# Spectral mixing and SwiGLU on one core: the first batch's first Fourier step kept in SBUF, re/im interleaved in the intermediates, last sums on VectorE

## The chip, the cores and the metric

The kernel runs on one NeuronCore of a Trainium2 chip. The metric is the device time of one execution in microseconds, as a median over runs. Before the change it is 3045.3 us (3043.2 to 3047.6, 3 runs).

## The reference, cut to what matters

```python
def _attn_ref(x, filt_r, filt_i):            # x: 8 x 3008 x 256
    X = np.fft.rfft(x, axis=1)
    Y = X * (filt_r + 1j * filt_i)[None]
    return np.fft.irfft(Y, n=x.shape[1], axis=1).astype(np.float32)

def _moe_ref(x, w_gate, w_val, w_out):       # 24064 tokens, 256 -> 1536 -> 256
    g = x @ w_gate
    return ((g / (1.0 + np.exp(-g))) * (x @ w_val) @ w_out).astype(np.float32)
```

The weights come in as float64. The kernel rounds them to float32 itself, in 36 "halves" of 128 x 256 numbers.

## The kernel before: the parts concerned

The transform of a batch runs in steps of matmuls: step one over 47 points, middle steps (a, product with the filter, b) over 64 points for 24 frequencies in 12 units of two, and the last step, which yields `y`. Between them stand two intermediates in DRAM, `d1` and `d2`. Batch one does all this before the main part can start; for batches two to eight the same steps are woven into the products of the batch before, each in the schedule of a group (one round of gate, value and output products).

```python
        def stage1(self, u):                      # step one, 16 of them
            ...
            pin(nc.tensor.matmul(out=ps[0:NK], lhsT=wf_t, rhs=self.x.pop(u), ...))
            yield
            pin(nc.scalar.copy(out=t1, in_=ps[0:NK]))
            queue = nc.scalar if self.b else nc.gpsimd
            pin(queue.dma_start(out=self.d1_rows[:, ts(u, NV), :], in_=t1))

        def load_two(self, u):                    # input of the middle steps
            ...
            for p in range(2):                    # real part, imaginary part
                a0 = p * NS + NV * u
                self.load(out=self.t2[u][64 * p:64 * p + 64],
                          in_=self.d1[a0:a0 + NV].rearrange("s n c -> n s c"))

        def stage2b(self, u):                     # end of the middle steps
            ...
            pin(nc.scalar.copy(out=g, in_=ps))
            for p in range(2):
                a0 = p * NS + NV * u
                queue = nc.scalar if self.b else (nc.sync, nc.gpsimd)[p]
                pin(queue.dma_start(out=self.d2[a0:a0 + NV].rearrange("s n c -> n s c"),
                                    in_=g[64 * p:64 * p + 64]))
```

For the later batches the two stores of `stage2b` stand in ScalarE's own order.

A rounding takes VectorE (two bit operations), ScalarE (two activations), VectorE again (three operations) and GpSimd (two to four), with its two intermediates `pw` and `w`.

In the lines of the profile PE is TensorE, PEld its weight loads, DVE VectorE, ACT ScalarE, POOL GpSimd and SP SyncE; a q behind the name means the engine's sequencer. `out<-in` names the tiles. `wpa` to `wpd` (`pa` to `pd` for later batches) are results of the Fourier steps, `wk`, `wa` and `we` those of the gate and value products, `wA`, `wF` and `wG` those of the output products; `f`, `c`, `m` and `o` are copies of such results (`f` with its sign changed) that ScalarE makes; `room`, `t` and `lent` are buffers in SBUF, `d` the intermediates in DRAM.

Of the kernel before, what the change touches and what calls it, by code (L numbers as in the profile page):

```python
# [93 lines left out]

LAST = "W1 o1 W2 o2 W6 o6 W5 o5 W3 o3 x0.o x1.o x2.o W7 o7 W4 o4 x3.o x4.o x5.o".split()
BLOCKS = (0, 1, 3, 2)
# [11 lines left out]
def dft_tables():  # L108
# [3 lines left out]
    w = np.stack([np.cos(ph), -np.sin(ph)], 1)  # L112
    wf = np.zeros((N1, 2, 2, NS, 2))
    wi = np.zeros((2, NS, 2, N1, 2))

    v = np.stack([2 * np.cos(ph), -2 * np.sin(ph)], 0)
    v[0, :, 0], v[1, :, 0] = 1.0, 0.0
    for h in range(2):
        wf[:, h, :, :, h] = w
        wi[:, :, h, :, h] = v.transpose(0, 2, 1) / S  # L120

# [18 lines left out]
def kernel(  # L140
# [13 lines left out]
    wi_dram = nc.inline_tensor(wi_host, name="wi_tbl")  # L154
    de_dram = nc.inline_tensor(de_host, name="de_tbl").ap()

    def pool(name, bufs, space=None):
# [36 lines left out]

    off_t = cpool.tile([128, 1], FP32)
    nc.vector.memset(off_t, -896.0)

    def filter_parts():
# [53 lines left out]
    NRAW = 3  # L252
    N_EARLY = 8

    def load_weights(i):
        if i in raws or i >= len(weights):
            return
        if i < N_EARLY:
            raws[i] = early_raw(i)
        else:  # L260
            raws[i] = rpool.tile([128, 2, 128, 2], U32, name=f"raw_{i}", tag="raw", bufs=NRAW)
        queue = nc.sync if i < N_EARLY else nc.scalar
        pin(queue.dma_start(out=raws[i], in_=weights[i][0]))

    def round_half(i):
# [14 lines left out]
        pin(nc.scalar.activation(out=w, in_=man, func=AF.Copy, scale=2.0 ** -20, bias=1.0))  # L280
        pin(nc.scalar.activation(out=pw, in_=pw, func=AF.Relu, bias=off_t))

        load_weights(i + NRAW - 1)
        yield
        pin(v.tensor_scalar(out=pw, in0=pw, scalar1=255.0, scalar2=2.0 ** 23,
                            op0=ALU.min, op1=ALU.mult))
        pin(v.scalar_tensor_tensor(out=pw.rearrange(flat), in0=raw.rearrange(flat2)[:, :, 1],
# [5 lines left out]
        e = nc.gpsimd  # L293
        pf = pw.bitcast(FP32)
        if use == "proj":
# [73 lines left out]
    def fbank(name):  # L369
        return fps.tile([128, NV, C], FP32, name=name, tag="f")  # L370

    def warm():


        banks = [bank("idle") for _ in range(NB)]
        for n in (512, 512, TQ, 2 * TQ):
            for ps in banks:
                pin(nc.tensor.matmul(
                    out=ps[:, 0:n], lhsT=wt_t[:, 0, 0, :],
                    rhs=wt_t[:, 0:2].rearrange("p s z f -> p (s z f)")[:, 0:n],  # L380
                    start=True, stop=True))

    class Spectral:
# [10 lines left out]
        def load(self, **kw):  # L394
            pin(nc.sync.dma_start(**kw))

        def place(self, tag, u):
            return lend(tag, u) if self.b else early(tag, u)

        def load_x(self, u):  # L400
            if self.b == 0:
                rows = x[0].rearrange("(r n) c -> r n c", n=32)
                for a, n in ((0, NV), (NV, 8 - NV)) if u == 0 else ((0, 8),):
                    for r in (slice(0, 80), slice(80, NR)):
                        self.load(out=x0[u][r, a:a + n, :],
                                  in_=rows[r, 8 * u + a:8 * u + a + n, :])
                for j in range(8 // NV):
                    self.x[8 // NV * u + j] = x0[u][:, ts(j, NV), :]
            elif u < N_ONE:
                self.x[u] = xpool.tile([NR, NV, C], FP32, name=f"x_{self.b}_{u}", tag="x")  # L410
                rows = x[self.b].rearrange("(r n) c -> r n c", n=32)

                for r in (slice(0, 80), slice(80, NR)):
                    self.load(out=self.x[u][r], in_=rows[r, ts(u, NV), :])

        def load_two(self, u):
            if u < N_TWO:
                b = self.b
                if b:
                    self.tb[u] = lend("tb", u).rearrange("p i (k c) -> p i k c", k=2)  # L420
                    self.load(out=self.tb[u], in_=de_dram[:, ts(u, NV)])

                    f = lend("f", u).rearrange("p (k i) c -> p k i c", k=2)
                    self.f[u] = f
                    for rows, view in filter_parts():
                        r, part = rows.start, rows.start // 64
                        for at in (r, r + 64) if part == 0 else (r,):
                            self.load(out=f[at:at + 32, part], in_=view(NV * u, NV))
                self.t2[u] = self.place("t2", u)
                for p in range(2):  # L430
                    a0 = p * NS + NV * u
                    self.load(out=self.t2[u][64 * p:64 * p + 64],
                              in_=self.d1[a0:a0 + NV].rearrange("s n c -> n s c"))

# [19 lines left out]
        def stage1(self, u):  # L454

            p1 = spool0 if self.b == 0 and u % 2 else t1pool
            t1 = p1.tile([NK, NV, C], FP32, name=f"t1_{self.b}_{u}", tag="t1", bufs=2)
            ps = self.bank(f"pa_{self.b}_{u}")
            pin(nc.tensor.matmul(out=ps[0:NK], lhsT=wf_t, rhs=self.x.pop(u),  # L459
                                         start=True, stop=True))  # L460
            if self.b:
                self.load_x(u + 3)
            yield
            pin(nc.scalar.copy(out=t1, in_=ps[0:NK]))
            queue = nc.scalar if self.b else nc.gpsimd
            pin(queue.dma_start(out=self.d1_rows[:, ts(u, NV), :], in_=t1))

        def stage2a(self, u):

            ahead = 1 if self.b else 3  # L470
            self.load_two(u + ahead)
            t2, f = self.t2.pop(u), self.f.pop(u)
# [25 lines left out]
        def stage2b(self, u):  # L498
# [8 lines left out]
            pin(nc.scalar.copy(out=g, in_=ps))  # L507
            for p in range(2):
                a0 = p * NS + NV * u
                queue = nc.scalar if self.b else (nc.sync, nc.gpsimd)[p]  # L510
                pin(queue.dma_start(out=self.d2[a0:a0 + NV].rearrange("s n c -> n s c"),  # L511
                                    in_=g[64 * p:64 * p + 64]))

# [52 lines left out]
    class Group:  # L566
# [89 lines left out]
        def project(self, op, last=False):  # L656
# [3 lines left out]
            if kind == "x":  # L660
                if q == NG - 1:
                    i, t = divmod(p, len(TOK))
                    skip = TOK[1] + 128 - TOK[2] if t == 2 else 0
                    rows = out[b * S:(b + 1) * S].rearrange("(r n) c -> r n c", n=32)
                    queue = (nc.sync, nc.scalar, nc.gpsimd)[t] if last else nc.gpsimd
                    pin(queue.dma_start(
# [40 lines left out]
    with tc.tile_pool(name="start", bufs=1) as spool0:  # L707
# [6 lines left out]
        units += [y_f[:, ts(i, NV * C)].rearrange("p (i c) -> p i c", c=C) for i in range(6)]  # L714
        early_places = {"p": (0, 5), "t2": (5, 4), "g": (9, 4), "q": (13, 3), "fr": (16, 3)}

# [4 lines left out]
        def early_raw(i):  # L721

            t, a = (tb0, i) if i < 4 else (f0, i - 4)
            t = t[:, 16 + 2 * a:18 + 2 * a]
            t = t.rearrange("p s k f -> p (s k f)" if i < 4 else "p s c -> p (s c)")
            return t.bitcast(U32).rearrange("p (b f two) -> p b f two", b=2, two=2)

        pin(nc.sync.dma_start(out=wf_t, in_=wf_dram.ap()))
        for i, n in enumerate((0, 2, 2, 4)):
            spec.load_x(i)  # L730
            for _ in range(n):
                load_weights(len(raws))
        for i in range(2):
            spec.load_tables(i)
        pin(nc.sync.dma_start(out=wi_t, in_=wi_dram.ap()))
        for u in range(N_ONE):
            run(spec.stage1(u))
            if u in (7, 8, 10, 11, 13, 14, 15):
                round_next()
        for _ in range(2):  # L740
            round_next()
        for u in range(3):
            spec.load_two(u)
        spec.load_tables(2)
        for i, j in PAIRS:
            combine_weights(0, i, j)
        for u in range(3):
            spec.real_part(u)
        lag = 3
        for u in range(N_TWO + lag):  # L750
            if u < N_TWO:
                run(spec.stage2a(u))
                spec.real_part(u + 3)
            if u >= lag:
                run(spec.stage2b(u - lag))
    for i in range(2):
        spec.load_t4(0, i)
    following = Spectral(1)
    for u in range(3):
        following.load_x(u)  # L760
    warm()
    for _ in range(8):
        round_next()
    for step in range(4):
# [3 lines left out]
    for piece in range(len(PIECES)):  # L768
        keep_weights(0, piece)

    hpool = pool("hp", 4)
# [7 lines left out]
    for b in range(B):  # L779
# [26 lines left out]
        for step in range(NCHUNK * NG + (b == B - 1)):  # L806
# [19 lines left out]
            for token in SCHEDULE:  # L826
# [12 lines left out]
                else:  # L839
                    g0 = before if old else this  # L840
                    if g0 is not None:
                        g0.step(op, nc.vector if ghost and op[0] == "S" and op[2] == "1" else None)
                if old or this is None:
# [19 lines left out]
    for op in LAST:  # L863
        older.project(op, True)
# [28 lines left out]
```

## Time and profile before

| part of the span | from, to (us) | length |
|---|---|---|
| start, up to the first product of the third group | 0 to 212.5 | 212.5 |
| steady stretch, up to the first of the last output products | 212.5 to 3017.9 | 2805.3 |
| last output products and sums | 3017.9 to 3032.9 | 15.0 |
| from the last sum to the end of the span | 3032.9 to 3043.3 | 10.4 |

Two lines of TensorE in order of time (start, duration, engine, line, operation, tiles, shapes, count) give the two cuts of the steady stretch before:

```profile
212.54 0.80 PE L600 MATMUL wk<-y,wt_t 128*128 128x188 f32 x4
...
3017.85 1.50 PE L677 MATMUL wA<-wo_t,h 128*128 128x128 f32 x12
```

### The profile page before, as it was taken

How to read it: one execution, taken by the hardware profiler on the slowest of the kernel's cores; microseconds unless marked ns; L12 is line 12 of the kernel's file. 1: busy time of each engine (PE TensorE's matmuls, PEld its weight loads, DVE VectorE, ACT ScalarE, POOL GpSimd, SP SyncE). 2: the span in 40 equal slices, each digit the busy share in tenths (PEclk: the TensorE clock that was granted, in tenths of full speed). 3: DMA queues.
4: the chain of work that ended last, by engine and by line, in shares of the span. 5: the costliest groups of instructions: out<-in, count | busy, mean ns of one | idle time of the engine just before them, and what ended most of it. 6: DMA issues, size and time to landing. Idle time of an engine off the chain costs nothing.

```text
span 3043.3 us, 57524 instructions
## 1 busy us (share of the span) xinstructions
PE 2948.7 (97%) x20152; PEld 2827.3 (93%) x20152; DVE 1923.5 (63%) x4407; ACT 1581.1 (52%) x4130; POOL 1599.7 (53%) x1797
## 2 busy tenths in 40 slices
PE   5779999999999999999999999999999999999998
PEld 2579999999999999999999999999999999999997
DVE  4686766566665666557665576655666566666665
ACT  3455455555455555555555545555545555555553
POOL 4665655454645455545554555545554545555553
PEclk9889999999999999999999999999999999999999
DMA  8645755556645656456655575555665566644442
GB/s 235 184 143 198 225 185 180 177 189 192 210 154 185 200 191 209 152 185 205 195 173 186 172 227 175 181 182 181 204 203 160 178 199 192 196 147 154 144 131 72
DMA packets 209739, 551.76 MB, mean 181 GB/s; under 512 B 32502, under 2 KB 104438, under 8 KB 208594
## 3 DMA queue, kind: packets, MB, share of 16 engines
q1 hardware_dynamic: 155724, 467.57, 48.5%
q10 hardware_dynamic: 43104, 51.66, 5.9%
q0 software_dynamic: 10624, 28.85, 3.0%
q8 instruction: 162, 2.65, 0.4%
q14 instruction: 125, 1.02, 0.1%
HBM read 462.76 MB, written 85.20 MB: 180 GB/s over the span
## 4 chain that ended last, share of the span: by engine, by line
PE 89%; ACT 1%; issue 1%; DMA 1%; DVE 1%; POOL 1%; ACTq 0%; POOLq 0%; DVEq 0%
PE wa L600 23%; PE wA L677 16%; PE wk L600 15%; PE we L600 12%; PE wG L677 8%; PE wF L677 4%; PE pd L522 3%; PE pa L459 3%; PE pb L476 2%; PE pc L503 2%; DMA out_dram<-o 1%; ACTq L511 0%; ACT lent L507 0%; POOL h L213 0%; ACT y_t L561 0%
## 5 line engine op out<-in xcount | busy, mean ns | idle before, releaser
L600 PE MATMUL wa<-y_t,wt_t 128*128 128x188 f32 x4560 | 902.5, 324 | 7.4 <-ACT wa L626 4.7
L600 PEld LDWEIGHTS wa<-y_t,wt_t 128*128 128x128 f32 x4560 | 749.0, 191 | 34.1 <-issue 15.8
L213 POOL TENSOR_TENSOR h<-h 128x376 f32<-128x376 f32 x191 | 183.4, 981 | 834.9 <-DVE h L647 834.9
L600 PE MATMUL wk<-y,wt_t 128*128 128x188 f32 x3040 | 586.2, 326 | 17.4 <-ACT f L615 11.4
L677 PE MATMUL wA<-wo_t,h 128*128 128x128 f32 x4608 | 580.0, 276 | 9.5 <-DVE o L213 6.1
L677 PEld LDWEIGHTS wA<-wo_t,h 128*128 128x128 f32 x4608 | 564.2, 192 | 24.3 <-issue 14.4
L216 POOL TENSOR_TENSOR h<-h 128x376 f32<-128x376 f32 x573 | 556.9, 993 | 0.6
L600 PEld LDWEIGHTS wk<-y,wt_t 128*128 128x128 f32 x3040 | 493.2, 192 | 49.9 <-issue 22.6
L600 PE MATMUL we<-y_t,wt_t 128*128 128x188 f32 x2280 | 441.4, 323 | 0.0
L216 DVE TENSOR_TENSOR we<-we,m 128x376 f32<-128x376 f32 x576 | 318.2, 555 | 186.9 <-PE we L600 128.4
L600 PEld LDWEIGHTS we<-y_t,wt_t 128*128 128x128 f32 x2280 | 377.1, 190 | 1.3 <-DVE we L220 0.7
L220 DVE SCALAR_TENSOR_TENSOR y<-wk,c 128x376 f32<-128x376 f32 x480 | 244.5, 542 | 153.6 <-ACT we L631 104.3
L216 POOL TENSOR_TENSOR D<-f,f 128x376 f32<-128x376 f32 x288 | 279.8, 985 | 113.7 <-ACT f L615 113.0
L635 ACT COPY m<-wa 128x376 f32<-128x376 f32 x576 | 272.7, 473 | 77.9 <-PE wa L600 76.8
L642 ACT ACTIVATE g<-wa 128x188 f32<-128x188 f32 x576 | 187.1, 327 | 200.4 <-PE wa L600 199.6
L677 PE MATMUL wG<-wo_t,h 128*128 128x128 f32 x2304 | 288.8, 275 | 0.7 <-DVE o L213 0.7
L677 PEld LDWEIGHTS wG<-wo_t,h 128*128 128x128 f32 x2304 | 282.1, 192 | 0.9 <-issue 0.9
L642 ACT ACTIVATE u<-we 128x188 f32<-128x188 f32 x576 | 189.4, 329 | 177.7 <-DVE we L216 157.2
L615 ACT ACTIVATE f<-wk 128x376 f32<-128x376 f32 x288 | 139.9, 486 | 253.9 <-PE wk L600 214.3
L622 DVE SCALAR_TENSOR_TENSOR x<-wk,f 128x376 f32<-128x376 f32 x192 | 104.5, 544 | 237.4 <-PE wk L600 236.5
L619 ACT COPY c<-wk 128x376 f32<-128x376 f32 x288 | 136.3, 473 | 223.7 <-PE wk L600 222.1
L631 ACT COPY we<-y 128x376 f32<-128x376 f32 x480 | 223.5, 487 | 50.6 <-issue 28.2
(119 smaller groups left out, 3833.6 us busy)
## 6 DMA issues: line engine op xcount, KB each, us to landing
wt_t<-w_all SPq DMA_DIRECT2D x186, 896.0 KB
wt_t<-w_all SPq DMA_DIRECT2D x186, 768.0 KB
t<-d SPq DMA_DIRECT2D x64, 384.0 KB
d<-t ACTq DMA_DIRECT2D x112, 192.0 KB
lent<-de_tbl SPq DMA_DIRECT2D x84, 256.0 KB
lent<-in_filt_r_dram SPq DMA_DIRECT2D x336, 64.0 KB
lent<-d SPq DMA_DIRECT2D x168, 128.0 KB
d<-lent ACTq DMA_DIRECT2D x168, 128.0 KB
```

Of the source, the lines that this page charges most:

```text
L213: return eng.tensor_tensor(out=dst, in0=a, in1=b, op=ALU.add)
L216: return eng.tensor_tensor(out=dst, in0=a, in1=b, op=ALU.subtract)
L220: return nc.vector.scalar_tensor_tensor(out=dst, in0=a, scalar=-1.0, in1=b, op0=ALU.mult, op1=ALU.subtract)
L459: pin(nc.tensor.matmul(out=ps[0:NK], lhsT=wf_t, rhs=self.x.pop(u), start=True, stop=True))
L600: pin(nc.tensor.matmul(out=ps[:, z], lhsT=self.wt[:, SLOT[p], z], rhs=rhs, start=start and z == 0, stop=True, skip_group_check=True))
L615: pin(act.mul(self.small(f"f{i}", f"f{i}", 1), t[f"k{i}"], -1.0))
L619: pin(act.copy(out=self.small(f"c{i}", f"c{i}", 1), in_=t[f"k{i}"]))
L622: pin(v.scalar_tensor_tensor(out=dst, in0=t[f"k{j}"], scalar=-1.0, in1=t[f"f{i}" if j == 3 else f"D{at}"], op0=ALU.mult, op1=ALU.add))
L631: pin(act.copy(out=self.bank(f"e{at}"), in_=t[f"y{at}"]))
L635: pin(act.copy(out=self.small(f"m{at}", "m", 4), in_=t[f"a{at}"]))
L642: pin(act.activation(out=self.small(op, "g", 3, 1)[:, 0], in_=ps[:, 1], func=AF.Silu))
L677: pin(nc.tensor.matmul(out=self.tiles[at][:, t, :], lhsT=self.hs[i][:, HID[p], t0:t0 + 128], rhs=wo_t[:, JB * q + i, WO[p], :], start=star ...
```

## The change

Its aim is the start: the first batch's intermediate `d1` no longer goes to DRAM and back. Step one is done with operands swapped, so that channels lie on partitions; the result stays in SBUF, and TensorE transposes it for the middle steps. SBUF so freed and DMA so spared let raw weights be loaded further ahead; roundings and weight combinations are reordered, and one rounding operation moves from VectorE to ScalarE. Since the transposes want real and imaginary part of one frequency side by side, both intermediates are laid out that way for all batches, and a unit's two transfers of 64 partitions become one of 128. At the end the eight last sums go to VectorE and the last stores to the two hardware queues.

```diff
+        def twos(self, d, u):
+            a = 2 * NV * u
+            return d[a:a + 2 * NV].rearrange("(s p) n c -> s (p n) c", p=2).rearrange(
+                "s q c -> q s c")
 ... load_two (batches two to eight)
-                for p in range(2):
-                    a0 = p * NS + NV * u
-                    self.load(out=self.t2[u][64 * p:64 * p + 64],
-                              in_=self.d1[a0:a0 + NV].rearrange("s n c -> n s c"))
+                self.load(out=self.t2[u], in_=self.twos(self.d1, u))
 ... stage2b
-            for p in range(2):
-                a0 = p * NS + NV * u
-                queue = nc.scalar if self.b else (nc.sync, nc.gpsimd)[p]
-                pin(queue.dma_start(out=self.d2[a0:a0 + NV].rearrange("s n c -> n s c"),
-                                    in_=g[64 * p:64 * p + 64]))
+            queue = nc.scalar if self.b else nc.sync
+            pin(queue.dma_start(out=self.twos(self.d2, u), in_=g))
 ... first batch
+                    pin(nc.tensor.matmul(out=ps[:, i], lhsT=x0[u // 2][:, u % 2 * 4 + i, ts(cb, 128)],
+                                         rhs=wf_t, start=True, stop=True))
 ...
+                    pin(nc.tensor.transpose(out=ps[:, i, ts(cb, 128)],
+                                            in_=one_t[:, cb, ts(NV * u + i, 128)], identity=unit_t))
 ... rounding
-        pin(nc.scalar.activation(out=pw, in_=pw, func=AF.Relu, bias=off_t))
+        pin(nc.scalar.activation(out=pf, in_=pw, func=AF.Relu, bias=off_t))
+        pin(nc.scalar.activation(out=pf, in_=pf, func=AF.Relu, bias=top_t, scale=-1.0))
+        pin(nc.scalar.activation(out=pw, in_=pf, func=AF.Copy, scale=-(2.0 ** 23), ...))
-        pin(v.tensor_scalar(out=pw, in0=pw, scalar1=255.0, scalar2=2.0 ** 23, ...))
 ... last stores
-                    queue = (nc.sync, nc.scalar, nc.gpsimd)[t] if last else nc.gpsimd
+                    queue = (nc.sync, nc.scalar)[(p + i) % 2] if last else nc.gpsimd
 ... (order of the start, early loads of raw weights, idle matmuls, last sums: cut)
```

More of the change, by code (lines that the diff above doesn't have):

```diff
@@ L93 @@
 KS = (-1, 0, 1, 2)
-LAST = "W1 o1 W2 o2 W6 o6 W5 o5 W3 o3 x0.o x1.o x2.o W7 o7 W4 o4 x3.o x4.o x5.o".split()
+LAST = """
+S00 S01 S10 S11 W1 o1 W2 o2 S20 S21 S30 S31 W6 o6 W5 o5 W3 o3 x0.o x1.o x2.o W7 o7 W4 o4 x3.o x4.o
+x5.o
+""".split()
 BLOCKS = (0, 1, 3, 2)
@@ L112, in dft_tables @@
     w = np.stack([np.cos(ph), -np.sin(ph)], 1)
-    wf = np.zeros((N1, 2, 2, NS, 2))
-    wi = np.zeros((2, NS, 2, N1, 2))
+    wf = np.zeros((N1, 2, NS, 2, 2))
+    wi = np.zeros((NS, 2, 2, N1, 2))
     v = np.stack([2 * np.cos(ph), -2 * np.sin(ph)], 0)
@@ L118, in dft_tables @@
     for h in range(2):
-        wf[:, h, :, :, h] = w
-        wi[:, :, h, :, h] = v.transpose(0, 2, 1) / S
+        wf[:, h, :, :, h] = w.transpose(0, 2, 1)
+        wi[:, :, h, :, h] = v.transpose(2, 0, 1) / S
     kap = np.where(q[:, None] < 32, s + N1 * q[:, None], s + N1 * (95 - q[:, None]))
@@ L155 @@
     de_dram = nc.inline_tensor(de_host, name="de_tbl").ap()
+    unit_dram = nc.inline_tensor(np.eye(128, dtype=np.float32), name="unit_tbl")
     def pool(name, bufs, space=None):
@@ L195 @@
     off_t = cpool.tile([128, 1], FP32)
+    top_t = cpool.tile([128, 1], FP32)
     nc.vector.memset(off_t, -896.0)
+    nc.vector.memset(top_t, 255.0)
     def filter_parts():
@@ L252 @@
     NRAW = 3
-    N_EARLY = 8
+    N_EARLY = 16
     def load_weights(i):
@@ L261, in load_weights @@
             raws[i] = rpool.tile([128, 2, 128, 2], U32, name=f"raw_{i}", tag="raw", bufs=NRAW)
-        queue = nc.sync if i < N_EARLY else nc.scalar
+        queue = nc.sync if i < 9 else nc.scalar
         pin(queue.dma_start(out=raws[i], in_=weights[i][0]))
@@ L280, in round_half @@
         pin(nc.scalar.activation(out=w, in_=man, func=AF.Copy, scale=2.0 ** -20, bias=1.0))
-        pin(nc.scalar.activation(out=pw, in_=pw, func=AF.Relu, bias=off_t))
+        pf = pw.bitcast(FP32)
+        pin(nc.scalar.activation(out=pf, in_=pw, func=AF.Relu, bias=off_t))
+        pin(nc.scalar.activation(out=pf, in_=pf, func=AF.Relu, bias=top_t, scale=-1.0))
+        pin(nc.scalar.activation(out=pw, in_=pf, func=AF.Copy, scale=-(2.0 ** 23),
+                                 bias=255 * 2.0 ** 23))
         load_weights(i + NRAW - 1)
         yield
-        pin(v.tensor_scalar(out=pw, in0=pw, scalar1=255.0, scalar2=2.0 ** 23,
-                            op0=ALU.min, op1=ALU.mult))
         pin(v.scalar_tensor_tensor(out=pw.rearrange(flat), in0=raw.rearrange(flat2)[:, :, 1],
@@ L293, in round_half @@
         e = nc.gpsimd
-        pf = pw.bitcast(FP32)
         if use == "proj":
@@ L370, in fbank, with idle @@
         return fps.tile([128, NV, C], FP32, name=name, tag="f")
+    def idle(t, banks, n):
+        for ps in banks:
+            pin(nc.tensor.matmul(out=ps[:, 0:n], lhsT=t[:, 0:128], rhs=t[:, 0:n],
+                                 start=True, stop=True))
     def warm():
         banks = [bank("idle") for _ in range(NB)]
-        for n in (512, 512, TQ, 2 * TQ):
-            for ps in banks:
-                pin(nc.tensor.matmul(
-                    out=ps[:, 0:n], lhsT=wt_t[:, 0, 0, :],
-                    rhs=wt_t[:, 0:2].rearrange("p s z f -> p (s z f)")[:, 0:n],
-                    start=True, stop=True))
+        for n in (TQ, 2 * TQ):
+            idle(wt_t[:, 0:2].rearrange("p s z f -> p (s z f)"), banks, n)
     class Spectral:
@@ L406, in load_x @@
                                   in_=rows[r, 8 * u + a:8 * u + a + n, :])
-                for j in range(8 // NV):
-                    self.x[8 // NV * u + j] = x0[u][:, ts(j, NV), :]
             elif u < N_ONE:
@@ L417, in load_two @@
             if u < N_TWO:
-                b = self.b
-                if b:
-                    self.tb[u] = lend("tb", u).rearrange("p i (k c) -> p i k c", k=2)
-                    self.load(out=self.tb[u], in_=de_dram[:, ts(u, NV)])
-                    f = lend("f", u).rearrange("p (k i) c -> p k i c", k=2)
-                    self.f[u] = f
-                    for rows, view in filter_parts():
-                        r, part = rows.start, rows.start // 64
-                        for at in (r, r + 64) if part == 0 else (r,):
-                            self.load(out=f[at:at + 32, part], in_=view(NV * u, NV))
-                self.t2[u] = self.place("t2", u)
-                for p in range(2):
-                    a0 = p * NS + NV * u
-                    self.load(out=self.t2[u][64 * p:64 * p + 64],
-                              in_=self.d1[a0:a0 + NV].rearrange("s n c -> n s c"))
+                self.tb[u] = lend("tb", u).rearrange("p i (k c) -> p i k c", k=2)
+                self.load(out=self.tb[u], in_=de_dram[:, ts(u, NV)])
+                f = lend("f", u).rearrange("p (k i) c -> p k i c", k=2)
+                self.f[u] = f
+                for rows, view in filter_parts():
+                    r, part = rows.start, rows.start // 64
+                    for at in (r, r + 64) if part == 0 else (r,):
+                        self.load(out=f[at:at + 32, part], in_=view(NV * u, NV))
+                self.t2[u] = lend("t2", u)
+                self.load(out=self.t2[u], in_=self.twos(self.d1, u))
         def load_tables(self, i):
@@ L454, in stage1 @@
         def stage1(self, u):
-            p1 = spool0 if self.b == 0 and u % 2 else t1pool
-            t1 = p1.tile([NK, NV, C], FP32, name=f"t1_{self.b}_{u}", tag="t1", bufs=2)
+            t1 = t1pool.tile([NK, NV, C], FP32, name=f"t1_{self.b}_{u}", tag="t1", bufs=2)
             ps = self.bank(f"pa_{self.b}_{u}")
@@ L460, in stage1, with stage1_first, turn @@
                                          start=True, stop=True))
-            if self.b:
-                self.load_x(u + 3)
+            self.load_x(u + 3)
             yield
             pin(nc.scalar.copy(out=t1, in_=ps[0:NK]))
-            queue = nc.scalar if self.b else nc.gpsimd
-            pin(queue.dma_start(out=self.d1_rows[:, ts(u, NV), :], in_=t1))
+            pin(nc.scalar.dma_start(out=self.d1_rows[:, ts(u, NV), :], in_=t1))
+        def stage1_first(self, u):
+            for cb in range(2):
+                ps = bank(f"pa_{u}_{cb}")[:, 0:4 * NK].rearrange("p (n k) -> p n k", k=NK)
+                for i in range(4):
+                    pin(nc.tensor.matmul(out=ps[:, i], lhsT=x0[u // 2][:, u % 2 * 4 + i, ts(cb, 128)],
+                                         rhs=wf_t, start=True, stop=True))
+                copy = (nc.scalar.copy, nc.vector.tensor_copy)[cb]
+                dst = one_t[:, cb].rearrange("p (k n) -> p n k", n=32)
+                pin(copy(out=dst[:, ts(u, 4)], in_=ps))
+        def turn(self, u):
+            if u >= N_TWO:
+                return
+            ps = self.bank(f"pt_{u}")
+            for i in range(NV):
+                for cb in range(2):
+                    pin(nc.tensor.transpose(out=ps[:, i, ts(cb, 128)],
+                                            in_=one_t[:, cb, ts(NV * u + i, 128)],
+                                            identity=unit_t))
+            self.t2[u] = early("t2", u)
+            pin(nc.scalar.copy(out=self.t2[u], in_=ps))
         def stage2a(self, u):
-            ahead = 1 if self.b else 3
-            self.load_two(u + ahead)
+            if self.b:
+                self.load_two(u + 1)
             t2, f = self.t2.pop(u), self.f.pop(u)
@@ L714 @@
         units += [y_f[:, ts(i, NV * C)].rearrange("p (i c) -> p i c", c=C) for i in range(6)]
-        early_places = {"p": (0, 5), "t2": (5, 4), "g": (9, 4), "q": (13, 3), "fr": (16, 3)}
+        early_places = {"p": (0, 5), "t2": (5, 3), "g": (9, 4), "q": (13, 3), "fr": (16, 3)}
+        zero = units[8].rearrange("p i c -> p (i c)")
+        one_t = lent[:, 0:2 * NK * 32].rearrange("p (b k) -> p b k", b=2)
+        spare = []
+        n = 0
+        while n < NPR - 1:
+            pair = ORDER[n][0] in "ABE" and ORDER[n + 1][0] in "ABE"
+            spare += [n] if pair else []
+            n += 2 if pair else 1
         def early(tag, u):
@@ L721, in early_raw @@
         def early_raw(i):
-            t, a = (tb0, i) if i < 4 else (f0, i - 4)
-            t = t[:, 16 + 2 * a:18 + 2 * a]
-            t = t.rearrange("p s k f -> p (s k f)" if i < 4 else "p s c -> p (s c)")
+            t = wt_t[:, spare[i]:spare[i] + 2].rearrange("p s z f -> p (s z f)") if i < 8 else \
+                wo_f[:, ts(i - 8, 512)]
             return t.bitcast(U32).rearrange("p (b f two) -> p b f two", b=2, two=2)
+        unit_t = spool0.tile([128, 128], FP32, name="unit")
+        pin(nc.scalar.dma_start(out=unit_t, in_=unit_dram.ap()))
+        pin(nc.vector.memset(zero, 0.0))
+        idle(zero, [bank("idle") for _ in range(5)], 512)
         pin(nc.sync.dma_start(out=wf_t, in_=wf_dram.ap()))
@@ L732 @@
                 load_weights(len(raws))
-        for i in range(2):
+        for i in range(3):
             spec.load_tables(i)
         pin(nc.sync.dma_start(out=wi_t, in_=wi_dram.ap()))
-        for u in range(N_ONE):
-            run(spec.stage1(u))
-            if u in (7, 8, 10, 11, 13, 14, 15):
+        for u in range(8):
+            spec.stage1_first(u)
+            if u in (4, 5, 6, 7):
                 round_next()
-        for _ in range(2):
-            round_next()
-        for u in range(3):
-            spec.load_two(u)
-        spec.load_tables(2)
-        for i, j in PAIRS:
-            combine_weights(0, i, j)
+        idle(tb0.rearrange("p s k c -> p (s k c)"), [bank("idle") for _ in range(4)], 512)
+        for u in range(2):
+            spec.turn(u)
         for u in range(3):
             spec.real_part(u)
+        for _ in range(4):
+            round_next()
         lag = 3
@@ L751 @@
             if u < N_TWO:
+                spec.turn(u + 2)
                 run(spec.stage2a(u))
@@ L755 @@
                 run(spec.stage2b(u - lag))
+            if 2 < u < 11:
+                load_weights(len(raws))
     for i in range(2):
@@ L760 @@
         following.load_x(u)
+    for _ in range(3):
+        round_next()
+    for i, j in PAIRS:
+        combine_weights(0, i, j)
+    for _ in range(2):
+        round_next()
     warm()
-    for _ in range(8):
-        round_next()
     for step in range(4):
@@ L769 @@
         keep_weights(0, piece)
+    for _ in range(4):
+        round_next()
     hpool = pool("hp", 4)
@@ L840 @@
                     g0 = before if old else this
-                    if g0 is not None:
-                        g0.step(op, nc.vector if ghost and op[0] == "S" and op[2] == "1" else None)
+                    if g0 is not None and not (ghost and op[0] == "S"):
+                        g0.step(op)
                 if old or this is None:
@@ L863 @@
     for op in LAST:
-        older.project(op, True)
+        if op[0] == "S":
+            older.step(op, nc.vector)
+        else:
+            older.project(op, True)
 _INS = ['x', 'filt_r', 'filt_i', 'moe_w_gate', 'moe_w_val', 'moe_w_out']
```

## The prediction

> **What bounds the kernel now.** I read the page first (busy shares, then the 40 slices), then the stretches of the first 100 us, then each engine in order of time around the places where TensorE stands still, and last the final 30 us.
>
> ```profile
> PE 2948.7 (97%) x20152; PEld 2827.3 (93%) x20152; DVE 1923.5 (63%) x4407; ACT 1581.1 (52%) x4130; POOL 1599.7 (53%) x1797
> PE   5779999999999999999999999999999999999998
> ```
>
> From the fourth slice on (228 us) TensorE is full: that is the steady part, some 2,800 us, whose matmuls the change leaves alone. Only the first three slices and the last can give anything. A complete wait list of TensorE over the first 240 us:
>
> ```profile
> PE wpb L476 <- DMA room<-d: 29.7, 5, 20.3
> PE wk L600 <- ACT f L615: 14.7, 5, 6.5
> PE wpa L459 <- DMA wo_t<-in_x_dram: 7.3, 2, 6.4
> PE wk L600 <- DVE y L213: 6.0, 1, 6.0
> ```
>
> The largest wait, 29.7 us, is what the change is aimed at: the first batch's step one is written to DRAM (d<-t) and read back (room<-d) before the middle steps. In order of time:
>
> ```profile
> 28.12 7.03 PE L459 MATMUL wpa<-x,wf_t 94*96 94x512 f32 x8
> 55.49 4.57 PE L476 MATMUL wpb<-room,tb 128*128 128x256 f32 x12 [20.33 <-DMA room<-d]
> 67.39 2.04 PE L476 MATMUL wpb<-room,tb 128*128 128x256 f32 x4 [7.33 <-DMA room<-d]
> 92.76 18.83 PE L378 MATMUL widle<-wt_t 128*128 128x512 f32 x56
> 121.13 1.62 PE L600 MATMUL wk<-y,wt_t 128*128 128x188 f32 x4 [5.99 <-DVE y L213]
> ```
>
> Step one ends at 35.2, the middle steps start at 55.5, and the first product of the main part at 121.1. But between 92.8 and 121 TensorE does idle work and one short step: somebody else sets the pace. VectorE shows who:
>
> ```profile
> 89.61 0.69 DVE L487 TENSOR_TENSOR y_t<-wpb,f 64x512 f32<-64x512 f32 x1
> 90.33 0.29 DVE L276 TENSOR_SCALAR w<-raw 128x256 uint32<-128x256 uint32 x1
> 106.81 0.29 DVE L276 TENSOR_SCALAR w<-raw 128x256 uint32<-128x256 uint32 x1 [3.04 <-DMA raw<-in_moe_w_gate_dram]
> 114.77 0.29 DVE L276 TENSOR_SCALAR w<-raw 128x256 uint32<-128x256 uint32 x1 [3.14 <-DMA raw<-in_moe_w_gate_dram]
> 120.58 0.49 DVE L213 TENSOR_TENSOR y<-wpd,y 128x188 f32<-128x188 f32 x1 [1.26 <-ACT y L534]
> ```
>
> The middle steps leave VectorE at 90.3; then eight roundings of float64 weight halves go through a VectorE-ScalarE-GpSimd loop until 119.2, and only behind them, in program order, the step that yields y. So the start is bound by a chain: loads, step one, DRAM round trip, middle steps, eight roundings, y, first group. What counts is how far the whole chain moves, not the 20 us gap alone.
>
> **What the Trainium skill says.**
> - "TensorE: Matmul & The Clock Gate", Part 1: after an idle window of about 3.4 us the array runs at half clock until about 3.4 us of activity. The trace agrees: the two passes of a 94x512 matmul start 0.86 us apart in step one, and take 0.86 us together once warm (208.60, the chain of waits). The column of granted clock says 1.00 in step one all the same, so it does not show this state.
> - "DMA: Bandwidth & Descriptors", Specifications: the HBM limit per core is about 358 GB/s. The trace reaches 354 in its best 10 us (20 to 30), with the DMA engines' share at 1.05: the loads of the start run near a limit.
> - "ScalarE: Activation LUTs", What ACT_TABLE_LOAD costs: an ACTIVATE is 186 ns + 0.833 ns per element, and about 93 ns more with a bias from a tile. For 256 elements 399 and 492 ns; the trace has 0.42 and 0.50 us for the two activations of a rounding.
> - "TensorE: Matmul & The Clock Gate", Part 4: a 128x128 transpose in bf16 takes 275 to 390 ns, and transposes do not count as activity for the clock. No run here has one yet, and none of float32.
>
> **The change, part by part.**
>
> *Loads.* The DRAM write (16 x 192 KB = 3.1 MB) and the read back (another 3.1 MB) go. Before the middle steps there remain x 3.1 MB, eight weight halves 2.1 MB and three tables of 2.1 MB, 11.5 MB. The windows give 1.66 MB in the first 10 us and 277 to 354 GB/s after; at an estimated 300, x is in at 1.66 + 0.3(t - 10) = 4.15 (x with four halves), t = 18 us; the first table (7.3 MB) at 29; the last at 43.
>
> *Step one.* 64 matmuls of 96 moving columns with 128 stationary ones, in place of 16 of 512. The nearest row is the last Fourier step, 32 records of 96*128 96x94 in 3.71 us, two for a matmul: 0.23 us each warm. 64 x 0.23 = 15 us, against 27.4 us (32 x 0.857, cold) now. Five idle matmuls at the start hold it warm, but it waits for x: I expect its end at about 22 us instead of 35. That is 13 us, which I do not count, since the next thing waits for the table.
>
> *Start of the middle steps.* Four idle matmuls need the first table (29), then the turns of units 0 and 1 (two copies of 0.58), six copies of the filter's real part (6 x 0.63), which wait for the same table, and then, behind them on ScalarE, four roundings. Those go at the pace of the loop: now 3.07 us each where nothing else waits (95.93 to 99.00). So 29 + 4.5 (idle, half cold) + 1.2 + 3.8 + some 9.5 for the roundings = 48 us for the first VectorE product, which is at 57.9 now.
>
> *Middle steps.* VectorE needs 2.16 us a unit (three products of 0.7). ScalarE now needs per unit 1.26 + 0.59; the change adds the copy of a turn, 0.58, and from unit 3 to 10 a DMA issue of 0.37: 2.8 us, so it becomes the bound in about six units. 3 x 2.16 + 6 x 2.8 + 3 x 2.16 = 30 us. They end at 78 on VectorE instead of 90.3: 12 us gained. The stall of 5 us that the trace has at 64 to 69 (room<-d) is in this.
>
> *Behind them.* Now: eight roundings in 28.9 us, of which 8.0 us are waits for raw weights. After: three roundings, the six weight combinations (on VectorE some 8 us now, at 49.7 to 58, hidden in the DRAM wait; on GpSimd 12 operations of 0.8, so about 9 to 10 us for the pair), then two roundings. With raw weights loaded ahead: 5 x 2.9 + 9 = 23 us. y starts 6 to 7 us sooner relative to the middle steps. But four roundings now come after y, ahead of the first group's VectorE work: 4 x 2.9 = 11.6 us given back. Net -5.
>
> *The rounding itself.* One VectorE operation (0.2 us from start to start) becomes two activations (0.50 + 0.41 us) on ScalarE. The loop VectorE, GpSimd, VectorE gets 0.2 us shorter; ScalarE's extra 0.9 us fits into a round. Over the 19 roundings that fall into the crowded stretch after 126 us, where VectorE is 80% busy, I allow 3 us, with the head start TensorE gets on products that wait for nothing.
>
> *Warming.* 14 idle matmuls of 512 columns go (14 x 0.86 = 12 us of TensorE). TensorE waits for VectorE there, so nothing.
>
> *The end.* Now:
>
> ```profile
> 3023.45 1.58 PE L677 MATMUL wA<-wo_t,h 128*128 128x128 f32 x12 [2.75 <-DVE o L213]
> 3019.10 3.74 DVE L216 TENSOR_TENSOR h<-h 128x376 f32<-128x376 f32 x3
> 3032.31 0.56 DVE L213 TENSOR_TENSOR o<-o,wA 128x384 f32<-128x384 f32 x1 [1.70 <-PE wA L677]
> ```
>
> Four sums on GpSimd (0.98 each) and four on VectorE hold up the output sums and so the third product until 3023.45. All eight on VectorE at 0.47 us from start to start, with the output sums between them: first four done at 3020.4, o1 at 3020.9, W6 at 3020.9 instead of 3023.45. Through o5 (3024.4), W3 (3025.8), o3, W7 (3027.1), o7, W4 (3029.3) the last output sum ends at 3030.1 instead of 3032.9: 2.8 us. The last stores leave GpSimd's queue for the two hardware queues: two issues of 0.6 us on one of them, about even.
>
> *Sum.* -12 (middle steps) + 5 (behind them) - 3 (rounding, head start) - 3 (end) = -13 us. My table landing at 29 us is on the careful side, so I put -15: 3030 us.
>
> **The rivals.**
> 1. *The DRAM trip's gain comes through whole.* If the four early roundings do not sit behind the table and the combinations hide behind GpSimd and ScalarE, the first group starts about 25 us sooner: 3018. For it: 20.3 us of pure wait go. Against: program order on ScalarE, and the combinations lose the wait they were hidden in.
> 2. *Another wait takes its place entirely.* The tables pace the middle steps, or TensorE falls cold between the idle matmuls and the loop, so that eight passes and four transposes take over 4 us a unit for the first few. The middle steps then end near 86, and with +5 behind them only the end is gained: 3040. For it: 11.5 MB at 300 GB/s is 43 us whatever TensorE does; transposes may not keep the clock.
> 3. *ScalarE becomes the bound in the crowded stretch* through its 0.9 us a rounding, delaying f, m and g that TensorE waits for (14.7 us on f now). This would cost up to 19 x 0.9 = 17 us: 3045. Against it: ScalarE's 52% share and its idle times there.
>
> **Range and chances.** The sum's uncertain terms are the start of the middle steps (5 us either way), their pace (4) and the given-back roundings (5); the steady part repeats within 0.2%. 3015 to 3041 us should hold it 8 in 10. A gain of 2% is 61 us, over four times the sum and more than the DRAM waits, y wait and end together, so hardly possible; a loss of 2% would need the steady part to suffer. Faster 0.02, within 2% 0.97, slower 0.01.
>
> **What would show it.** Step one's last matmul near 22 us; no room<-d at all; the first product of the middle steps on VectorE near 48 and its last near 78, with ScalarE full between; combinations between the third and fourth rounding behind them; y near 101; four roundings between y and the first group; third product of the end 2.5 us sooner. Wrong would be: a first middle product before 42 or after 54, waits on tables inside the loop, middle steps at 3 us a unit or more, or a steady part that changed its length.

## The result, and the profile after

The changed kernel takes 3011.7 us (3010.4 to 3013.4, 4 runs), against 3044.3 us for the kernel before in the same rounds: ratio 0.9894, interval 0.9877 to 0.9911. Within 2%, as forecast, but the gain is 33 us, where 15 were predicted and 3015 was the lower end of the range.

The two cuts of the steady stretch in the changed kernel, from TensorE in order of time:

```profile
202.62 0.80 PE L626 MATMUL wk<-y,wt_t 128*128 128x188 f32 x4
...
2991.83 1.50 PE L703 MATMUL wA<-wo_t,h 128*128 128x128 f32 x12
```

With them the table by parts, from the two profiled runs:

| part | before | after | gain | predicted |
|---|---|---|---|---|
| start | 212.5 | 202.6 | 9.9 | 10 |
| steady stretch | 2805.3 | 2789.2 | 16.1 | 0 |
| last products and sums | 15.0 | 12.5 | 2.5 | 3 |
| last sum to end | 10.4 | 4.3 | 6.1 | 0 |

The last column adds up to the sum of 13 us; the prediction put 2 us on top, because it took its landing of the first table for cautious. So the start and the sums came near what was worked out (the start with some luck, see experiment 12), and 22 of the 35 us (spans of the profiles) lie where the prediction had put nothing. The start first. VectorE of the changed kernel in order of time:

```profile
48.21 0.68 DVE L512 TENSOR_TENSOR room<-wpb,y_t 128x512 f32<-128x512 f32 x1
...
74.81 0.69 DVE L516 TENSOR_TENSOR y_t<-wpb,f 64x512 f32<-64x512 f32 x1
75.53 0.29 DVE L282 TENSOR_SCALAR w<-wo_t 128x256 uint32<-128x256 uint32 x1
...
99.69 0.49 DVE L219 TENSOR_TENSOR y<-wpd,y 128x188 f32<-128x188 f32 x1 [1.70 <-ACT y L560]
```

The middle steps go from 48.2 to 75.5 (57.9 to 90.3 before), y follows at 99.7 (120.6 before). Then come the four roundings that were put behind y. The three largest of TensorE's waits in the first 240 us (us in total, times, longest) show what became of the DRAM wait:

```profile
PE wk L626 <- ACT f L641: 28.8, 5, 19.8
PE wpb L505 <- ACT room L495: 11.5, 1, 11.5
PE wk L626 <- DVE y L219: 10.2, 1, 10.2
```

No wait for a load from d is left, but the wait for ScalarE's f has grown from 14.7 to 28.8 us: ScalarE's first copy of a product now stands behind four more roundings. The 29.7 us of DRAM waits were for the most part exchanged for these three: 14.1 us more for f, 11.5 for the copy of a turn that stands behind four roundings on ScalarE, and 4.2 more for y.

The steady stretch is the surprise. The chain of waits of the kernel before, in order of time (start, duration, what), around one of its stalls:

```profile
825.57 5.71 DMA out_dram<-o
...
833.82 0.49 ACT lent L507
834.31 0.02 issue
834.33 0.58 ACTq L511
834.91 0.04 issue
834.95 1.34 ACTq L511
836.28 0.04 issue
836.33 0.49 ACT o L689
```

The stall begins with the late landing of an output store, for which ScalarE's copy into `o` at 831.38 waited 4.51 us. While ScalarE catches up, the two stores of one unit come: the issues alone take 0.58 and 1.34 us, and only then can ScalarE copy the output product that TensorE waits for. Over all 84 units the issues show as follows (count, then shortest/median/longest in ns, then first and last start), first before, then after:

```profile
L511 ACTq DMA_DIRECT2D d<-lent x168: 582/619/1532, 324.6 to 2654.1; - x168
```

```profile
L538 ACTq DMA_DIRECT2D d<-lent x84: 366/366/389, 316.1 to 2627.6; - x84
```

One transfer of 128 partitions is issued in 0.37 us, one of 64 in 0.62 us: a unit's issues fall from 1.24 to 0.37 us, 0.87 x 84 = 73 us of ScalarE's order. TensorE's waits from 230 to 2900 us were, before:

```profile
PE wa L600 <- ACT wa L626: 4.7, 8, 1.2
PE wk L600 <- ACT f L615: 2.0, 4, 0.8
PE wA L677 <- ACT o L689: 1.9, 4, 0.9
PE pb L476 <- DMA lent<-d: 0.7, 1, 0.7
PE wA L677 <- DVE o L213: 0.2, 1, 0.2
```

After, that list is empty. It adds up to 9.5 us, of 16.1 gained. (The list counts from the modelled end of a matmul, so it shows less than the delay: at 786.07 one of 0.63 us against the changed kernel's spacing stands in it as 0.47.) All this pointed to the merged transfers and was so far only a reading.

### The profile page after: what moved, and what is told of

Same layout as the page of the kernel before. It is cut to its first block, busy times and chain, and to the rows that moved or that the text cites. A ratio compares the mean times of both kernels' runs of the same rounds, so it can differ in the third digit from the quotient of the medians. Undisturbed runs are those within 1.5% of the kernel's fastest.

```text
span 3008.6 us, 57532 instructions
## 1 busy us (share of the span) xinstructions
PE 2930.9 (97%) x20286; PEld 2836.1 (94%) x20286; DVE 1920.6 (64%) x4385; ACT 1627.2 (54%) x4206; POOL 1578.4 (52%) x1763
## 4 chain that ended last, share of the span: by engine, by line
PE 92%; DVE 0%; ACT 0%; issue 0%; POOL 0%; ACTq 0%
PE wa L626 24%; PE wA L703 17%; PE wk L626 16%; PE we L626 12%; PE wG L703 8%; PE wF L703 4%; PE pd L548 3%; PE pa L465 3%; PE pb L505 2%; PE pc L532 2%; DVE o L219 0%; DVE pw L284 0%; DVE y L226 0%; DVE h L222 0%; DVE h L219 0%
```

## The experiments

Each was run in five rounds beside the kernel before, whose medians in the three jobs were 3045.3, 3046.2 and 3047.0 us. "Stretch" is the steady stretch as cut above, from the run's profile; start and end as in the table.

**1. The changed kernel with both transfers split again (batches two to eight).**

```diff
-                self.load(out=self.t2[u], in_=self.twos(self.d1, u))
+                for p in range(2):
+                    self.load(out=self.t2[u][64 * p:64 * p + 64], in_=self.half(self.d1, u, p))
 ... stage2b
+            if self.b:
+                for p in range(2):
+                    pin(nc.scalar.dma_start(out=self.half(self.d2, u, p),
+                                            in_=g[64 * p:64 * p + 64]))
```

> The changed kernel, but in batches two to eight each unit's intermediate goes out and comes back in two transfers of 64 partitions again, as before. Theory A (the 16 us that the steady part lost are the merged transfers, through ScalarE's issue time): about 3027 us, and stalls of ScalarE behind d<-lent return. Rival B (the steady part gained by its earlier start, or by other things that moved in the schedule): 3012 us as the changed kernel.

3028.7 us, ratio 0.9952 (0.9938 to 0.9965); stretch 2807.0. The whole steady gain is gone, start and end keep theirs. Rival B falls, and theory A holds as far as the merged transfers are the cause; that ScalarE's issue time is the way it works is tested only in experiments 5 to 7.

**2. The kernel before with the new layout and merged transfers alone** (tables with re/im inside s, `twos` for batches two to eight; the first batch still goes through DRAM).

> The kernel before with re/im inside s and the merged transfers in batches two to eight alone. Theory A: 3029 us, ratio 0.995, with TensorE's shift growing by some 2.4 us per batch and nothing gained in the first 230 us. Rival B: 3044 us.

3027.1 us, ratio 0.9939 (0.9927 to 0.9952); stretch 2788.2, start 210.8. From the other side the same: the steady gain needs nothing else of the change.

**3. The changed kernel with the last stores on the old queues.**

```diff
-                    queue = (nc.sync, nc.scalar)[(p + i) % 2] if last else nc.gpsimd
+                    queue = (nc.sync, nc.scalar, nc.gpsimd)[t] if last else nc.gpsimd
```

> The changed kernel with the last six stores on the three queues of before, GpSimd's among them. Theory A (a store on GpSimd's queue at the very end lengthens the end): 10.4 us again between the last output sum and the end of the span instead of 4.3, so 3018 us. Rival B (the end is shorter for another reason, for instance that the tail's data come sooner): 4.3 us stay, 3012 us.

3016.4 us, ratio 0.9904 (0.9890 to 0.9917). By time alone the intervals of this and of the changed kernel overlap; the profile decides. Its end (engines in order of time), and three of its windows (busy time of PE, PEld, DVE, ACT and POOL, then granted clock, DMA share, GB/s):

```profile
3005.63 0.55 DVE L219 TENSOR_TENSOR o<-o,wA 128x384 f32<-128x384 f32 x1 [1.70 <-PE wA L703]
3006.48 0.58 POOL L692 DMA_DIRECT2D out_dram<-o  x1 [2.98 <-DVE o L219]
```

```profile
3008.00:3010.00 2.00, 0.00 (x0) 0.00 (x0) 0.00 (x0) 0.00 (x0) 0.00 (x0) 0.66 0.40 114
3010.00:3012.00 2.00, 0.00 (x0) 0.00 (x0) 0.00 (x0) 0.00 (x0) 0.00 (x0) 0.50 0.00 0
3012.00:3014.00 2.00, 0.00 (x0) 0.00 (x0) 0.00 (x0) 0.00 (x0) 0.00 (x0) 0.50 0.00 0
```

From the last sum (ends 3006.2) to the end of the span (3014.6) it takes 8.4 us, against 4.3 in the changed kernel and 10.4 in the kernel before. The data have landed by 3010; the last 4.6 us move nothing. So GpSimd's queue at the very end costs about 4 us here (6 between the two original kernels, and in experiment 4; the 2 us between are not explained), and it isn't the transfer. What runs in that time the profile does not show; that stays open.

**4. The kernel before with the new ending alone** (last sums on VectorE, two queues).

> The kernel before with the new ending alone: all eight last sums on VectorE, last stores on the two hardware queues. Theory A: 2.5 us from the sums and 6 us from the queue, 3036 us. Rival B: the sums alone, 3042 us.

3036.7 us, ratio 0.9965 (0.9953 to 0.9978). Last sum to end: 4.3 us, first of the last products to last sum: 12.5. As theory A has it.

**5 and 6. Which of the two transfers?** The changed kernel with only the stores split, then with only the loads split (each half of the diff of experiment 1).

> The changed kernel with only the stores of the second intermediate in batches two to eight split into two transfers of 64 partitions, as before. Theory S (the issue of the second store holds up ScalarE, and with it TensorE): about 3028 us, the issue of d<-lent in the chain of waits again. Rival L (the loads matter, through the wait of the middle steps for lent<-d): 3012 us.

> The changed kernel with only the loads of the first intermediate in batches two to eight split in two. Theory S: 3012 us, no change. Rival L: about 3028 us.

Stores split: 3022.6 us, ratio 0.9925 (0.9913 to 0.9938), stretch 2798.3, issues of 0.62 us again, and eight of TensorE's waits back:

```profile
PE wa L635 <- ACT wa L661: 4.8, 8, 1.1
```

Loads split: 3013.8 us, ratio 0.9894 (0.9881 to 0.9908), stretch 2787.8. So the stores matter and the loads don't by themselves; but 9 us of the stretch are less than the 18 of experiment 1, and theory S had said all of it. Split loads cost about 9 us only where the stores are split too. Where this second half arises can be read from the traces. Compare the starts of VectorE's output sums in experiment 1 and with the stores split alone, each counted from its first cut: of the 8.6 us between them, 6.5 come at four places, near 450, 830, 1920 and 2280 us. In experiment 1 the chain of waits has the landing of an output store (out_dram<-o) at the last three, 4.9 to 5.9 us long, as the kernel before has at 825.57; ScalarE falls behind there, and the two issues then stand ahead of its next copy. Near 450 us it has a store and two loads of the middle steps. With the stores split alone no such landing stands in it. Why split loads make these landings late is not shown, and no run tried it.

**7. Who issues, or what is transferred?** The same split stores, issued by SyncE.

```diff
-                    pin(nc.scalar.dma_start(out=self.half(self.d2, u, p),
+                    pin(nc.sync.dma_start(out=self.half(self.d2, u, p),
```

> The changed kernel with the stores of the second intermediate in batches two to eight in two halves, as in a_split_stores, but issued by SyncE instead of ScalarE. Theory S (what costs is ScalarE's time for the issue): the steady stretch stays at 2789 us or less, 3012 us, unless SyncE's own order delays the loads behind the stores. Rival D (two transfers of 64 partitions are slow or disturb others in the DMA engines, whoever issues them): 2798 us for the stretch as in a_split_stores, 3022 us.

3014.0 us, ratio 0.9894 (0.9880 to 0.9907); stretch 2789.4. On SyncE the two halves take as long to issue as they did on ScalarE:

```profile
L544 SPq DMA_DIRECT2D d<-lent x168: 575/596/1481, 321.4 to 2633.5; - x168
```

but they cost the stretch nothing beyond its spread (2787.8 to 2789.4 in the runs with merged stores). The same transfers, the same DMA engines; only ScalarE's order was relieved. Theory S holds for the stores, rival D falls.

**8. The rounding's fourth step back on VectorE** (the rounding part of the change undone).

> The changed kernel with the fourth step of the rounding back on VectorE and two activations less on ScalarE. Theory (as in my prediction, 0.2 us less in the loop of each rounding, 3 us in all for the move): 3015 us. Rival (ScalarE's extra 0.9 us per rounding costs as much or more in the crowded stretch): 3012 us or less.

3014.1 us, ratio 0.9895 (0.9882 to 0.9909), the same as the changed kernel's within the interval. Its start is 209.0 us, against 202.6 to 207.7 in the seven profiles whose start is the changed kernel's. So the move may be worth a few us, as the 3 us allowed for; these runs do not show it.

**9. Three buffers for the intermediates of a rounding.**

```diff
-        pw = rpool.tile([128, 2, 128], U32, name=f"pw_{i}", tag="pw", bufs=2)
-        w = rpool.tile([128, 2, 128], FP32, name=f"w_{i}", tag="w", bufs=2)
+        pw = rpool.tile([128, 2, 128], U32, name=f"pw_{i}", tag="pw", bufs=3)
+        w = rpool.tile([128, 2, 128], FP32, name=f"w_{i}", tag="w", bufs=3)
```

> The changed kernel with three buffers in place of two for the two intermediates of a rounding. Theory (a rounding waits for GpSimd's end of the one two before it, 3 us a turn; this loop sets the pace of the start): a turn falls towards 2 us, the first product after the roundings comes 10 us sooner, 3002 us. Rival (VectorE and ScalarE are as full anyway, or TensorE bounds the stretch behind): 3012 us.

3002.7 us, ratio 0.9860 (0.9845 to 0.9875). The roundings behind y on VectorE, in the changed kernel and with three buffers:

```profile
110.43 0.29 DVE L282 TENSOR_SCALAR w<-wo_t 128x256 uint32<-128x256 uint32 x1 [1.83 <-POOL lent L219]
...
113.43 0.29 DVE L282 TENSOR_SCALAR w<-wo_t 128x256 uint32<-128x256 uint32 x1 [1.58 <-POOL lent L219]
...
116.43 0.29 DVE L282 TENSOR_SCALAR w<-raw 128x256 uint32<-128x256 uint32 x1 [1.58 <-POOL lent L219]
```

```profile
105.73 0.67 DVE L282 TENSOR_SCALAR w<-wo_t 128x256 uint32<-128x256 uint32 x1
...
107.98 0.54 DVE L282 TENSOR_SCALAR w<-wo_t 128x256 uint32<-128x256 uint32 x1
...
110.10 0.54 DVE L282 TENSOR_SCALAR w<-raw 128x256 uint32<-128x256 uint32 x1
```

A round of 3.00 us becomes one of 2.2, and the waits for GpSimd are gone. This is the direct test of the prediction's main reading of the start, that a loop of VectorE and GpSimd sets its pace: the start shortens to 193.8 us, the stretch stays (2789.4).

**10. The four roundings ahead of the wait for the first table.**

```diff
+        for _ in range(4):
+            round_next()
         for u in range(2):
             spec.turn(u)
         for u in range(3):
             spec.real_part(u)
-        for _ in range(4):
-            round_next()
```

> The changed kernel with the four roundings before the middle steps ahead of the turns and of the copies of the filter's real part, which wait for the first table. Theory (they hold up the middle steps only since ScalarE does them after that wait): first product of the middle steps on VectorE at 43 instead of 48 us and everything after it 5 us sooner, 3007 us. Rival (table and transfers set the pace anyway, so the time comes back inside the loop as waits for tables): 3012 us.

3007.4 us, ratio 0.9873 (0.9859 to 0.9886); but the first product of the middle steps comes at 47.2, not 43, and the start of 201.7 is just below the spread of the unchanged starts. The time is as the theory said, the way there is not; inconclusive by itself. The trace shows why the middle steps hardly gained: the roundings now end on ScalarE at 44.2 us, still 3 us each, and only then come the turns and the copies of the filter, so it is the same work in another order.

**11. Three buffers and the roundings first.**

> Three buffers in the rounding loop and the four roundings first. If the two gains add: 3002 - 5 = 2997 us. If the roundings, being faster with three buffers, no longer hold up the start of the middle steps: 3002 us.

2997.1 us, ratio 0.9835 (0.9822 to 0.9849): faster than both kernels. Here the middle steps start at 42.8, and the start is 189.2 us. The two gains add.

**12. The changed kernel again**, beside the last three.

> The changed kernel once more, beside the others on one chip. Both theories: 3012 us; third group's first product (wk<-y,wt_t after 185) at 202 to 206 us, and 2789 us from there to the first of the last products (12 x wA at the end).

3012.4 us, ratio 0.9888 (0.9874 to 0.9901), start 204.3, stretch 2787.8. This sets the scale for the rest: the start varies by up to 5 us from profile to profile (so the 9.9 us of the first pair are at the high end; the seven starts have a mean of 204.9, against 211.5 for the three starts that are the kernel before's: a gain of about 7 us), the stretch by 1.6 us.

## Why the prediction was wrong

*Where it failed.* The step is in the first reading: "that is the steady part, some 2,800 us, whose matmuls the change leaves alone". The matmuls are left alone, and the change still shortened that part by 16 us, since it halves the number of the intermediates' stores and loads that ScalarE and SyncE issue there (168 to 84 each). The prediction had itself named "a steady part that changed its length" as a sign of being wrong. The merging stood in the diff and was given no term of the sum. The issue time was to be had: the trace of before has 168 issues of 0.62 us in ScalarE's order, and its chain of waits, in the list by line, names "ACTq L511" with 0.5% of the span, some 15 us. I took "full" for "nothing to gain". The 97% are of the whole span, and most of the missing 3% lies in the start: from 230 to 2900 us TensorE is busy in 2660.4 of 2670 us before and in all of it after. So the busy share alone, 9.6 us short of full, would not have told of 16 us; the chain of waits pointed at it. Experiments 1 and 2 show the cause from both sides, 5 and 7 that the stores alone make half of it (9 us), and that this half is ScalarE's time for the issue; the other half appears only with the loads split as well, and how it comes about stays open in part.

*The second failure* is a mis-sized term: the last stores, "about even". I counted issues and landings, and did not ask why the span before ended 7 us after the last data had moved. Measured 6.1 us between the two kernels and in experiment 4, 4.1 in experiment 3.

*What held.* The first product of the middle steps on VectorE: 48 foretold, 48.2 measured, with the terms behind the idle matmuls as foretold (turns 1.1 us against 1.2, copies of the filter 3.8 against 3.8, roundings 8.5 against 9.5). The term ahead of them agrees partly by luck: step one ended at 27.7 us in place of 22, as the last of x came at 21.6 and the clock was at half rate, and the idle matmuls begin at 28.71, a us behind it. In the profile of experiment 12 they follow step one at 30.77 without any wait, so there step one and not the table sets their start; when the table landed, the profiles do not show. The end of the middle steps: 78 against 75.5; the term for ScalarE as the bound (six units at 2.8 us) was too high, units kept VectorE's pace of 2.16 us but for one gap of 1.5 (66.87). y: 101 against 99.7. The roundings given back behind y, and with them a start that gains 10 us or less where the DRAM wait had promised 20 to 30, are there: the wait for f of up to 19.8 us is one place where the expected gain went, and in experiment 9, with faster roundings, it falls to 15.1 us. That the first pair gave 9.9 us where the sum has 10 is luck in part: over all profiles it is 7. The sums at the end: 2.8 against 2.5. (The prediction's "complete wait list" shows the four longest of twelve entries.)

*The rivals.* The first (whole DRAM trip gained, 3018) came nearer in time than the sum did, for the wrong reason: the start did not gain 25 us. The second (cold TensorE, tables as the pace) did not come: four passes take 2.07 us at 49.91, where the clock granted is 0.50, but 1.03 us from 53.9 on, and the middle steps end at 75.5, not near 86. The third (ScalarE's rounding work as the bound in the crowded stretch) can't be seen either way in experiment 8.

*The clock and the skill's pages.* The half rate that the prediction takes from "TensorE: Matmul & The Clock Gate", Part 1, is in the traces, but not its end. With idle matmuls ahead, the first 32 of step one's 64 matmuls took 7.28 us, 0.23 us each, the warm estimate; the last 16, behind a wait for x, took 6.13 us, 0.38 each, with a granted clock of 0.50 from 24 us on. And in the kernel before, step one's passes stay 0.86 us apart from 9.3 to 35.2 us without a break in TensorE's work, where the page has about 3.4 us of activity; two passes take 1.71 us also at 190.33, where the column says 0.50. So the prediction's "the trace agrees" holds for the rate and not for how soon it ends; why it lasted is open. "DMA: Bandwidth & Descriptors", Issuing engines are not separate DMA queues, says that issuing from several engines only saves the sequencer's time, "which is usually small relative to the DMA itself". The trace agrees that it is small (0.62 us to issue a half; the one median to landing that the profile gives for such a half, issued by GpSimd, is 3.0 us), and experiment 7 shows that the small time is worth 9 us when the sequencer is that of an engine which TensorE waits for.

## What to carry to other kernels

Before calling a stage "left alone", count every instruction that the diff removes from each engine's order there, DMA issues too: their time isn't in the busy share, and an engine at half load (ScalarE, 52%) can still be the one that is waited for. Here a store issued by ScalarE, which TensorE waits for, was better as one large one, or issued by SyncE. And removing the longest wait of a chain gains only what the next link allows: here a third buffer in the rounding loop was worth about 10 us more.

## What the Trainium skill lacked or had wrong

- "DMA: Bandwidth & Descriptors" has no figure for the issue time of a transfer on trn2 by its shape. Here two runs of 1 KB on each of 128 partitions take 0.37 us to issue and the same on 64 partitions 0.62 us (up to 1.5), on ScalarE and SyncE alike (SyncE 0.36 and 0.60): the smaller one is the dearer.
- The same page, Specifications, gives first-byte latencies of about 1 us for GpSimd's queue and 0.6 us for the hardware queues. A last store on GpSimd's queue lengthened the end by 4 to 6 us, most of it after the data had landed; no page read has that.
- "TensorE: Matmul & The Clock Gate", Part 4, has 275 to 390 ns for a 128x128 bf16 transpose. In float32 each takes 0.27 us here (median of 48), so no longer than the page's bf16; the page gives no rate for several in a row, and four of them between the middle steps' passes start 0.11 us apart (54.73 to 55.16 for four), with the passes next to them at the warm rate.
